# A long-convolution and MLP kernel: one filter block transformed by halves, two sums moved to accumulating DMAs, and a new instruction order

## The chip, the cores and the metric

The kernel runs on one core of one Trainium2 chip. The metric is the device time of one execution in microseconds. The kernel before took 238.65 us (median of three runs, 238.65 to 238.9).

A core has TensorE (PE; its weight loads are listed apart as PEld), VectorE (DVE), ScalarE (ACT), GpSimd (POOL) and SyncE (SP). They run side by side and wait for each other through semaphores. Plain DMAs are issued by SP here, and DMAs that add to what lies at the destination (accumulating DMAs) by POOL.

## The reference

The input is a sequence of 2048 tokens with 512 features, in bf16. Four layers follow each other, each added to its input: convolution, MLP, and the same two again with the same weights.

```python
def _A_ref(q, k, v, shift_k, ssm_k, ssm_D):
    ...
    for t in range(ks):                                    # ks = 4
        k_shift = k_shift + k_pad[:, t:t + S, :] * shift_k[:, ks - 1 - t][None, None, :]
    kv = k_shift * v
    ...                                                    # rfft over 2 S of kv and of ssm_k
    y_f = kv_f * kf_f[None, :, :, :]
    y = ...                                                # irfft, the first S tokens
    y = y + kv * ssm_D[None, None, :]
    return q * y

def _B_ref(x, w1, b1, w2, b2):
    y = _layernorm(x, axis=-1)
    h = _gelu(jnp.einsum("bsd,df->bsf", y, w1) + b1)       # 512 -> 1376
    return jnp.einsum("bsf,fd->bsd", h, w2) + b2

x = A_q
x = x + _A_ref(_layernorm(x, axis=-1), A_k, A_v, A_shift_k, A_ssm_k, A_ssm_D)
x = x + _B_ref(_layernorm(x, axis=-1), B_w1, B_b1, B_w2, B_b2)
x = x + _A_ref(_layernorm(x, axis=-1), A_k, A_v, A_shift_k, A_ssm_k, A_ssm_D)
x = x + _B_ref(_layernorm(x, axis=-1), B_w1, B_b1, B_w2, B_b2)
```

The convolution's result y depends on k, v and the filter only, not on x. So it is computed once and used in both layers.

## The kernel before

**Blocks.** The 2048 tokens are cut into four blocks of 512. Token t of a block lies on partition t // 4 in slot t % 4. The convolution is done block by block in the frequency domain: `spectrum_h(m)` makes the spectrum of filter block m (H0 to H3), `shift(b)` the short convolution of k and its product with v (S0 to S3), `forward` or `forward4` the spectrum of that (K0 to K3), `products(b)` the sum over j of X[j] times H[b-j] (P0 to P3), and `inverse(b)` the way back (Y0 to Y3). Each transform is a set of matmuls with a table of cosines and sines. Then `mlp(b, L)` follows for block b in layer L (called M00, M10, M01 and so on, block first): in its part a the normalisation, the gate with y and a second normalisation, in its part b the two matmuls with the gelu between.

**A transform in two ways.** `direct` makes each of four output tiles of 1024 columns from eight matmuls (four token slots, real and imaginary part, 512 columns each), and ScalarE's copy of a tile (`copy`, line 575) is the result. `forward` makes the even and the odd slots apart, with four matmuls a tile, and the results are the sum and the difference of two tiles: two more VectorE operations of 2048 elements when called with `whole`. Filter blocks 1 and 2 use `direct`, blocks 0 and 3 `forward`. The odd slots with the sign turned come from a copy of half the table that is negated once at the start (`negate`, line 636).

**Products.** A complex product is made of two multiplications on VectorE, one for the real and one for the imaginary part, each of 2048 elements (L569, the helper `tt`). The first term is written into the accumulator and each later term into one of three slots, from which an accumulating DMA of 512 KB (helper `accumulate`, L676) adds it. After the last term VectorE subtracts or adds the two halves of each sum and forms what the inverse transform reads.

`keep()` copies H1's spectrum (L730), then `wrap(m)` adds the block before to each filter spectrum: the real part on VectorE, the imaginary part by an accumulating DMA of 256 KB.

**The order.** The program lists some thousand operations with what they read and write. The tracker works in cells of four elements, and two operations that touch one cell of which one writes are put in order. An operation may have two possible engines: SIDE lists those that take their second choice. For copies of transposed tiles, the negation and the norms (`norm`, L860 on ScalarE, L861 on VectorE) the first choice is ScalarE and the second VectorE; for the small operations on statistics (`small`) it is VectorE and POOL. BANKS gives each PSUM tile its bank, and ORDER the order of all operations, from which each engine's own order follows. SIDE, BANKS and ORDER are the result of a search outside of the program with the durations written beside each operation; the chip takes from them only the order and the engines. `keep_busy` puts matmuls without a purpose (L1027) where that estimate has TensorE idle.

**Lines to follow.** L915: first matmul of an MLP, L920 its gelu, L949 (and L939) the second, L954 and L957 the residual sum, L829 and L831 statistics, L898 transposes ahead of an MLP, L591 all transforms, L714 the short convolution, L563 the transposition of short rows into columns, such as the bias b1. The row b1 is loaded to the start of `R_HT[0]`.

Of the kernel before, what the change touches and what calls it, by code (L numbers as in the profile page):

```python
# [366 lines left out]
def _tables():  # L367
# [8 lines left out]
SIDE = [27, 30, 36, 53, 118, 121, 129, 151, 220, 293, 300, 306, 364, 386, 496, 499, 517, 537, 581, 595, 730, 731, 741, 742, 752, 764, 827, 830, 844, 845, 848, 862, 866, 914, 915, 926, 929, 935, 936, 946, 947]  # L376
BANKS = "36424405320422044444020004461636165302046622145035042530020422242022432360231256613054243602540142362450404020024152406632314524121231045060153260200404000612503263500643350243511320451623164065313412554620212124626031532560"
ORDER = [
# [48 lines left out]
def bass_interleave_layers__ssm_conv_h3__mixer_channel_mlp__prompt_kernel(  # L427
        nc, A_q, A_k, A_v, A_shift_k, A_ssm_k, A_ssm_D, B_x, B_w1, B_b1, B_w2, B_b2, out):
    P = Prog(nc)
# [222 lines left out]
    def spectrum_h(m):  # L652
        o = R_BT + 4 * U * (m % 2)
        tl = Tile(P, 2)
        ins = [(i, c, A(0, 128, R_H[m] + c * U + i, [4, 128])) for i in range(4) for c in range(4)]

        def f(e, ins=ins, tl=tl):
            for i, c, src in ins:
                r = e.transpose(QB(tl, 0, 128, i * U + c * 128, [1, 128]), src, IDN)  # L659
            return r  # L660
        P.op(PE, f, 16 * 60.0, reads=[x[2] for x in ins] + [IDN], tile=tl)
        copy(A(0, 128, o, [1, 4 * U]), tl, lambda tl=tl: QB(tl, 0, 128, 0, [1, 4 * U]), 2048, (ACT, DVE), True)
        if m == 0:
            tt(A(0, 1, o, [1, U]), A(0, 1, o, [1, U]), A(0, 1, R_D, [1, U]), ALU.add, 512)
        if m in (1, 2):
            return direct(o, R_H[m])
        forward(o, R_H[m], (R_TMP, R_HT[0], R_EO[0], R_EO[0])[m], m > 0)
# [10 lines left out]
    def shift(b):  # L678
        kt = R_KT[b % 2]
        for z in range(2) if b == 0 else ():  # L680
# [8 lines left out]
            copy(A(0, 128, kt + 2 * 129 * z + 1, [4 * 129, 4], [129, 2], [1, 128]), tl, lambda tl=tl: QB(tl, 0, 128, 0, [256, 4], [128, 2], [1, 128]), 1024, (ACT, DVE), True)  # L689
        if b:  # L690
# [8 lines left out]
            copy(A(0, 128, kt + 1, [129, 16], [1, 128]), tl, lambda tl=tl: QB(tl, 0, 128, 0, [128, 16], [1, 128]), 2048, (ACT, DVE), True)  # L699
# [3 lines left out]
        for h in range(2):  # L703
            tl = Tile(P, 2)
            ins = []
            for z in range(2):
                c = 2 * h + z
                for m in (0, 1, 2, 3, -1, -2, -3):
                    ins.append((z * 512 + max(m, 0) * 128, A(0, 128, kt + (c * 4 + m % 4) * 129 + (m >= 0), [1, 128]),
# [31 lines left out]
    def products(b):  # L741

        for c in range(2):
# [15 lines left out]
            if b in ():  # L759
# [3 lines left out]
        for cs in ((0, 1),) if b else ((0,), (1,)):  # L763
            acc, n = R_ACC + cs[0] * 4096, len(cs)
            d = [[4096, 2]] if n == 2 else []
            for ri in range(1 if b in () else 2):
# [88 lines left out]
    def norm(b, i, mr, o):  # L855
# [6 lines left out]
        P.op((ACT, DVE), f, {ACT: 705.0, DVE: 330.0}, reads=[x, m, r], writes=[o])  # L862
# [195 lines left out]
```

## Time and profile before

| what | value |
|---|---|
| median of three runs | 238.65 us |
| the profiled execution | 238.38 us |
| its span, first to last instruction | 236.6 us |
| granted TensorE clock | 1.00 |
| VectorE 128x2048 bf16 sum or product (L569) | 1212 ns |
| ScalarE 128x1024 copy out of PSUM (L575) | 1030 ns |
| accumulating DMA, 512 KB and 256 KB, issue to landing | 5.4 and 4.3 us |

The profile is of one execution. A row of the chain of waits has a start, a length, and the engine and line that ran then. A row of the timeline has start and length of a run of like instructions, then engine, line, operation, output and input, count, and in brackets the idle time before it with what ended that. A row of the groups has the count, the busy time, the mean of one in ns, and the idle time before. The table by stage has the busy time and the number of instructions of PE, PEld, DVE, ACT and POOL, the granted clock, the busy share of DMA and its GB/s.

### The profile page before, as it was taken

To read this page: it belongs to the slowest core of one execution; us is meant where nothing else is said; L and a number is where in the kernel's file an instruction comes from. 1 tells how busy PE (TensorE), PEld (TensorE's weight loads), DVE (VectorE), ACT (ScalarE), POOL (GpSimd) and SP (SyncE) were. 2 spreads that over 40 slices of the span, in tenths; PEclk is the share of its full clock that TensorE was granted. 3 is DMA by queue.
4 is the path that set the end of the run, shared out by engine and by line. 5 is a ranking of instruction groups with operands and counts; after the bars stand their busy time and mean duration, and the time that the engine had idled before them with its cause. 6 is when DMAs were issued, how large, how long until landed. Compare 5 with 4: busy or idle time off the path is not lost.

```text
span 236.6 us, 3707 instructions
## 1 busy us (share of the span) xinstructions
PE 229.3 (97%) x1418; PEld 126.7 (54%) x1418; DVE 187.7 (79%) x366; ACT 168.0 (71%) x260; POOL 74.5 (31%) x93
## 2 busy tenths in 40 slices
PE   8999999999999999899999999899999999999995
PEld 4646645547746754345444544444457654447864
DVE  1669999999999999999999999789897414933022
ACT  2168779999999599989987965558938446815810
POOL 1000034257963454580367523334302101310000
PEclk9999999999999999999999999999999999999999
DMA  6999904989975987840299999940022220022016
GB/s 185 395 378 344 392 30 179 184 249 189 157 114 93 172 155 136 155 90 0 42 191 192 188 202 231 197 94 3 1 44 44 47 44 0 3 44 44 0 37 232
DMA packets 19865, 32.42 MB, mean 137 GB/s; under 512 B 7588, under 2 KB 13318, under 8 KB 19720
## 3 DMA queue, kind: packets, MB, share of 16 engines
q0 software_dynamic: 5808, 16.26, 36.4%
q1 hardware_dynamic: 14038, 15.93, 20.7%
q8 instruction: 11, 0.18, 0.3%
q14 instruction: 6, 0.05, 0.1%
q10 hardware_dynamic: 2, 0.00, 0.0%
HBM read 12.26 MB, written 2.10 MB: 61 GB/s over the span
## 4 chain that ended last, share of the span: by engine, by line
PE 55%; DVE 31%; DMA 6%; ACT 5%; issue 2%; DVEq 0%
DVE ar L569 22%; PE ps L949 21%; PE ps L915 18%; PE ps L591 7%; DMA ar<-ar 6%; DVE sm L829 5%; ACT ar L575 3%; PE ps L714 3%; PE ps L939 2%; PE ps L1027 2%; PE ps L659 1%; DVE ar L726 1%; ACT ar L920 1%; DVE ar L954 1%; DVE ar L957 1%
## 5 line engine op out<-in xcount | busy, mean ns | idle before, releaser
L569 DVE TENSOR_TENSOR ar<-ar 128x2048 bf16<-128x2048 bf16 (+2 forms) x129 | 115.4, 926 | 4.1 <-ACT ar L575 2.3
L915 PE MATMUL ps<-ar 128*128 128x256 bf16 (+3 forms) x484 | 80.1, 321 | 1.1 <-ACT ar L920 0.7
L920 ACT ACTIVATE ar<-ps,sm 128x256 bf16<-128x256 f32 (+3 forms) x121 | 61.4, 572 | 26.7 <-PE ps L915 26.4
L575 ACT ACTIVATE ar<-ps 128x1024 bf16<-128x1024 f32 (+2 forms) x61 | 63.7, 1098 | 17.9 <-PE ps L591 11.4
L949 PE MATMUL ps<-ar 128*128 128x512 bf16 (+1 forms) x330 | 75.7, 379 | 0.0
L915 PEld LDWEIGHTS ps<-ar 128*128 128x128 bf16 (+1 forms) x484 | 47.8, 100 | 32.5 <-ACT ar L920 1.4
L949 PEld LDWEIGHTS ps<-ar 128*128 128x128 bf16 (+1 forms) x330 | 31.9, 98 | 35.3 <-ACT ar L920 0.5
L676 POOL DMA_DIRECT2D ar<-ar x34 | 32.3, 1002 | 53.9 <-DVE ar L569 18.4
L591 PE MATMUL ps<-ar 128*128 128x512 bf16 x200 | 47.1, 379 | 1.0 <-DVE ar L726 0.5
L860 ACT ACTIVATE ar<-ar,sm 128x512 bf16<-128x512 bf16 x45 | 34.4, 808 | 7.5 <-DVE sm L818 7.4
L817 POOL TENSOR_TENSOR sm<-sm 128x2 f32<-128x2 f32 x32 | 29.1, 908 | 29.0 <-DVE sm L834 16.2
L829 DVE BATCH_NORM_STATS2 sm<-ar 128x6 f32<-128x512 bf16 x48 | 32.5, 685 | 1.7 <-DMA ar<-in_A_q_dram 1.5
L591 PEld LDWEIGHTS ps<-ar 128*128 128x128 bf16 x200 | 18.5, 98 | 24.0 <-ACT ar L575 2.3
L957 DVE TENSOR_TENSOR ar<-ps,ar 128x512 bf16<-128x512 f32 x14 | 9.6, 685 | 16.7 <-PE ps L949 16.6
L954 DVE SCALAR_TENSOR_TENSOR ar<-ps,ar 128x512 bf16<-128x512 f32 x16 | 10.9, 683 | 7.9 <-PE ps L949 7.8
L714 PE MATMUL ps<-ar 128*128 128x256 bf16 (+3 forms) x112 | 15.1, 288 | 0.3 <-DVE ar L576 0.3
L850 ACT ACTIVATE ar<-ar,sm 128x512 bf16<-128x512 bf16 x16 | 11.5, 722 | 4.3 <-DVE sm L846 4.1
L836 POOL TENSOR_SCALAR sm<-sm 128x2 f32<-128x2 f32 x4 | 3.7, 914 | 30.2 <-DVE sm L831 30.0
L714 PEld LDWEIGHTS ps<-ar 128*128 128x128 bf16 x112 | 9.6, 98 | 5.1 <-DVE ar L576 0.8
L846 POOL TENSOR_SCALAR sm<-sm 128x2 f32<-128x2 f32 x6 | 4.8, 792 | 12.2 <-DVE ar L954 11.9
L831 DVE BATCH_NORM_AGGREGATE sm<-sm 128x2 f32<-128x6 f32 x48 | 7.7, 172 | 0.2
L861 DVE TENSOR_SCALAR ar<-ar,sm 128x512 bf16<-128x512 bf16 x19 | 7.5, 408 | 0.2
(43 smaller groups left out, 78.2 us busy)
## 6 DMA issues: line engine op xcount, KB each, us to landing
ar<-ar POOLq DMA_DIRECT2D x24, 512.0 KB, 5.4
ar<-ar POOLq DMA_DIRECT2D x10, 256.0 KB, 4.3
ar<-in_A_ssm_k_dram SPq DMA_DIRECT2D x4, 512.0 KB, 10.3
ar<-in_A_v_dram SPq DMA_DIRECT2D x4, 512.0 KB, 5.7
ar<-in_A_q_dram SPq DMA_DIRECT2D x4, 512.0 KB, 10.1
ar<-in_A_k_dram SPq DMA_DIRECT2D x3, 512.0 KB, 7.4
out_dram<-ar SPq DMA_DIRECT2D x3, 512.0 KB, 3.7
ar<-in_B_w_dram SPq DMA_DIRECT2D x1, 1376.0 KB, 11.2
```

Of the source, the lines that this page charges most:

```text
L569: return P.op(DVE, lambda e: e.tensor_tensor(o, a, b, op), 66.0 + 0.52 * n, reads=[a, b], writes=[o])
L575: return e.activation(dst, src(), AF.Copy)
L591: r = e.matmul(Q(tl, 0, 128, ri * 512, [1, 512]), w, m, start=a, stop=z)
L676: P.op(POOL, lambda e: e.dma_start(dst, src, accum_op=ALU.add), 880.0, reads=[src, dst], writes=[dst], dma=True, nbytes=nb)
L714: r = e.matmul(Q(tl, 0, 128, q, [1, n]), w, d, start=a, stop=o)
L817: P.op(POOL, lambda e: e.tensor_tensor(r, v, hf, ALU.pow), 690.0, reads=[v, hf], writes=[r])
L829: P.op(DVE, lambda e, st=st, x=x: e.bn_stats(st, x), 600.0, reads=[x], writes=[st])
L860: return e.activation(o, x, AF.Identity, bias=m, scale=r)
L915: r = e.matmul(Q(tl, 0, rows, 0, [1, n]), w, m, start=dk == 0, stop=dk == 3)
L920: P.op(ACT, lambda e, dst=dst, tl=tl, rows=rows, bias=bias, n=n: e.activation(dst, Q(tl, 0, rows, 0, [1, n]), AF.Gelu_apprx_tanh, bias=bia ...
L949: r = e.matmul(Q(tl, 0, 128, 0, [1, 512]), ins[fc][0], ins[fc][1], start=fc == 0, stop=fc == 10)
L954: P.op(DVE, lambda e, x=x, tl=tl, mr=mr: e.scalar_tensor_tensor(x, Q(tl, 0, 128, 0, [1, 512]), 1.0, x, ALU.mult, ALU.add, accum_out=mr), 7 ...
```

## The change

Filter block 1 goes through `forward` instead of `direct`, with `R_HT[0]` as the place of the even and odd parts. For block 2 the sum of the two halves of the imaginary products is made by one accumulating DMA of 256 KB for each half of the frequencies, right behind that half's last product, in place of one VectorE addition of 2048 elements. The transposed k is laid by token slot first and column group second, where it was the other way round; the copies into it and the matmuls out of it follow. The duration of a norm on VectorE, as the search uses it, goes from 330 to 385 ns. SIDE, BANKS and ORDER are new; the numbers of the operations move with the added and removed ones.

```diff
-SIDE = [27, 30, 36, 53, 118, 121, 129, 151, 220, 293, 300, 306, 364, 386, 496, 499, 517, 537, 581, 595, 730, 731, 741, 742, 752, 764, 827, 830, 844, 845, 848, 862, 866, 914, 915, 926, 929, 935, 936, 946, 947]
+SIDE = [27, 51, 120, 131, 142, 153, 288, 305, 366, 388, 499, 517, 520, 584, 595, 606, 620, 733, 734, 745, 752, 755, 763, 766, 767, 833, 836, 854, 857, 858, 865, 868, 869, 917, 918, 932, 938, 939, 949, 950]
...
-        if m in (1, 2):
+        if m in (2,):
             return direct(o, R_H[m])
         forward(o, R_H[m], (R_TMP, R_HT[0], R_EO[0], R_EO[0])[m], m > 0)
...
-            copy(A(0, 128, kt + 2 * 129 * z + 1, [4 * 129, 4], [129, 2], [1, 128]), tl, lambda tl=tl: QB(tl, 0, 128, 0, [256, 4], [128, 2], [1, 128]), 1024, (ACT, DVE), True)
+            copy(A(0, 128, kt + 8 * 129 * z + 1, [129, 4], [4 * 129, 2], [1, 128]), tl, lambda tl=tl: QB(tl, 0, 128, 0, [256, 4], [128, 2], [1, 128]), 1024, (ACT, DVE), True)
...
-            copy(A(0, 128, kt + 1, [129, 16], [1, 128]), tl, lambda tl=tl: QB(tl, 0, 128, 0, [128, 16], [1, 128]), 2048, (ACT, DVE), True)
+            copy(A(0, 128, kt + 1, [129, 4], [4 * 129, 4], [1, 128]), tl, lambda tl=tl: QB(tl, 0, 128, 0, [512, 4], [128, 4], [1, 128]), 2048, (ACT, DVE), True)
...
-                    ins.append((z * 512 + max(m, 0) * 128, A(0, 128, kt + (c * 4 + m % 4) * 129 + (m >= 0), [1, 128]),
+                    ins.append((z * 512 + max(m, 0) * 128, A(0, 128, kt + (m % 4 * 4 + c) * 129 + (m >= 0), [1, 128]),
...
-            if b in ():
+            if b in (2,):
                 p, q = (A(0, 128, acc + 2048 + 512 * z, [1024, 2], [1, 512]) for z in range(2))
                 accumulate(p, q, 410000)
...
-            for ri in range(1 if b in () else 2):
+            for ri in range(1 if b in (2,) else 2):
                 p, q = (A(0, 128, acc + 2048 * ri + 512 * z, *d, [1024, 2], [1, 512]) for z in range(2))
...
-        P.op((ACT, DVE), f, {ACT: 705.0, DVE: 330.0}, reads=[x, m, r], writes=[o])
+        P.op((ACT, DVE), f, {ACT: 705.0, DVE: 385.0}, reads=[x, m, r], writes=[o])
```

More of the change, by code (lines that the diff above doesn't have):

```diff
@@ L373, in _tables @@
     return F.transpose(1, 0, 2, 3, 4).reshape(128, 2048), F.transpose(4, 2, 3, 0, 1).reshape(128, 2048) / 512
-SIDE = [27, 30, 36, 53, 118, 121, 129, 151, 220, 293, 300, 306, 364, 386, 496, 499, 517, 537, 581, 595, 730, 731, 741, 742, 752, 764, 827, 830, 844, 845, 848, 862, 866, 914, 915, 926, 929, 935, 936, 946, 947]
-BANKS = "36424405320422044444020004461636165302046622145035042530020422242022432360231256613054243602540142362450404020024152406632314524121231045060153260200404000612503263500643350243511320451623164065313412554620212124626031532560"
+SIDE = [27, 51, 120, 131, 142, 153, 288, 305, 366, 388, 499, 517, 520, 584, 595, 606, 620, 733, 734, 745, 752, 755, 763, 766, 767, 833, 836, 854, 857, 858, 865, 868, 869, 917, 918, 932, 938, 939, 949, 950]
+BANKS = "26424403120422040440042024260056342416310350522105601620040244242020261106404513132153164155521036001450404424024025555402536621364526035610402321444242200520245052163032651656442501653354104262100301532201443655366605256310"
 ORDER = [
[42 rows of a table removed]
[42 rows of a table added]
 ]
```

84 rows, old and new, of the table ORDER are left out of this document.

## The prediction

> **What bounds the kernel now.** I read the page first, then the chain of waits, then the table by stage, then who TensorE waits for, then the timeline at the joints.
>
> ```profile
> span 236.6 us, 3707 instructions
> ...
> PE 229.3 (97%) x1418; PEld 126.7 (54%) x1418; DVE 187.7 (79%) x366; ACT 168.0 (71%) x260; POOL 74.5 (31%) x93
> ```
>
> The chain that ended last goes: TensorE mixed with others to 33 us, VectorE to 91, TensorE to 131, VectorE and an accumulating DMA to 163, TensorE to the end. Two of its pieces:
>
> ```profile
> 147.72 7.50 DMA ar<-ar
> ...
> 195.75 9.50 PE ps L915 x44
> ```
>
> The last row gives the price of a matmul: 9.50 us / 44 = 0.216 us for 512 columns, with nothing between. Now the stages (first column: stretch, then its length, then busy time by engine):
>
> ```profile
> 33.00:98.00 65.00, 63.89 (x429) 36.55 (x426) 64.07 (x116) 59.90 (x85) 34.70 (x37) 1.00 0.77 157
> 98.00:132.00 34.00, 33.74 (x174) 15.87 (x175) 33.76 (x65) 29.34 (x46) 17.91 (x23) 1.00 0.58 109
> 132.00:164.00 32.00, 30.64 (x159) 14.30 (x158) 29.24 (x55) 20.89 (x33) 11.84 (x14) 1.00 0.77 159
> 164.00:234.00 70.00, 69.94 (x433) 42.35 (x431) 36.63 (x98) 39.31 (x82) 7.92 (x12) 1.00 0.17 43
> ```
>
> From 33 to 132 us TensorE and VectorE are both full; after 164 TensorE alone is, 69.94 of 70 us. So the time is TensorE's list of work plus the little it stands still. Two limits work at once: TensorE's total, and the joints where a convolution's products on VectorE (inverse transforms Y1, Y2, Y3) must be ready when TensorE's list comes to them. At each joint VectorE has just finished:
>
> ```profile
> 65.63 5.20 DVE L569 TENSOR_TENSOR ar<-ar 128x2048 bf16<-128x2048 bf16 x5
> ...
> 68.03 1.89 PE L591 MATMUL ps<-ar 128*128 128x512 bf16 x8
> ...
> 107.62 7.76 DVE L569 TENSOR_TENSOR ar<-ar 128x2048 bf16<-128x2048 bf16 x9
> ...
> 112.07 2.13 PE L591 MATMUL ps<-ar 128*128 128x512 bf16 x8
> ...
> 157.89 5.54 DVE L569 TENSOR_TENSOR ar<-ar 128x2048 bf16<-128x2048 bf16 x6
> ...
> 163.49 1.04 PE L591 MATMUL ps<-ar 128*128 128x512 bf16 x4
> ```
>
> Y1 starts at 68.03, right after the first two of the row from 65.63, block 1's last sums (2 x 1.2 us, to 67.95); Y2 at 112.07, inside the row from 107.62 (its first six instructions are block 2's sums); Y3 at 163.49, after the row that ends at 163.43.
>
> **The change part by part.** (a) *Filter block 1 by halves.* Four tiles of eight matmuls become four of four: 16 x 0.216 = 3.46 us less for TensorE, in the stretch of 25 to 33 us:
>
> ```profile
> 27.92 8.80 PE L591 MATMUL ps<-ar 128*128 128x512 bf16 x40
> ...
> 31.57 1.02 ACT L575 ACTIVATE ar<-ps 128x1024 bf16<-128x1024 f32 x1 [0.64 <-PE ps L591]
> ```
>
> ScalarE's copy of such a tile is 1.02 us and TensorE's eight matmuls 1.73 us, so ScalarE waited 0.64 us there; with 0.87 us a tile it no longer does. VectorE gains a sum and a difference of 2048 elements, two at 1.21 us (first row below): +2.42 us. The copy of the spectrum (keep) and block 1's wrap now wait for these two:
>
> ```profile
> L569 DVE TENSOR_TENSOR ar<-ar 128x2048 bf16<-128x2048 bf16 x60 | 71.5, 1212 | 1.9 <-DMA ar<-ar 1.3 <-ACT ar L575 0.5
> ...
> 34.64 0.76 POOL L730 DMA_DIRECT2D ar<-ar  x1 [1.52 <-ACT ar L575]
> ...
> 38.02 4.10 DVE L569 TENSOR_TENSOR ar<-ar 128x2048 bf16<-128x2048 bf16 x4 [0.47 <-ACT ar L575]
> ...
> 40.49 1.26 POOL L676 DMA_DIRECT2D ar<-ar  x1 [3.13 <-DMA ar<-ar]
> ...
> 48.02 1.21 DVE L569 TENSOR_TENSOR ar<-ar 128x2048 bf16<-128x2048 bf16 x1
> ```
>
> Keep issues at 34.64 now. In VectorE's new order the two sums stand just ahead of the K1 sums that begin at 38.02, so by estimate they end near 37 and keep issues 2.4 us later. The wrap follows keep by 40.49 - 34.64 = 5.85 us and its transfer of 256 KB takes 4.3 (a row under b): 37 + 5.85 + 4.3 = 47.2 us. Its first reader, block 1's product with this filter, begins at 48.02 and moves two places back. So it costs nothing, with 0.8 us of cover; from below it can't gain, and without the cover it is at most 2.4 - 0.8 = 1.6 us at Y1. The second wrap moves behind two small POOL operations of M00, and its reader stands eight VectorE operations after the first's: nothing.
>
> The intermediate lies where the row b1 is loaded, so two of the four tiles wait for b1's transposition, which the order moves ahead of them.
>
> ```profile
> 14.82 0.59 SPq L495 DMA_DIRECT2D ar<-in_B_b_dram  x2
> ...
> ar<-in_B_w_dram SPq DMA_DIRECT2D x1, 96.0 KB, 14.4
> ```
>
> b1 is issued by 15.4 us, right behind the 96 KB of W2 that took 14.4 us because of the 1280 KB ahead of them; the tiles come after 25 us. If b1 were as slow, 29.8 us, ScalarE would copy the other two tiles and H2's first: 0 to 1 us, I take 0.
>
> (b) *Block 2's imaginary sums.* One VectorE operation of 2048 elements goes, -1.21 us; two accumulating DMAs of 256 KB come.
>
> ```profile
> ar<-ar POOLq DMA_DIRECT2D x24, 512.0 KB, 5.4
> ar<-ar POOLq DMA_DIRECT2D x10, 256.0 KB, 4.3
> ...
> L676 POOL DMA_DIRECT2D ar<-ar x34: 853/902/1727, 40.5 to 153.0; - x34
> ...
> 95.62 0.87 POOL L676 DMA_DIRECT2D ar<-ar  x1 [2.07 <-DVE sm L852]
> ...
> 100.42 0.94 POOL L676 DMA_DIRECT2D ar<-ar  x1 [1.61 <-DMA ar<-ar]
> ...
> 106.37 1.22 DVE L569 TENSOR_TENSOR ar<-ar 128x2048 bf16<-128x2048 bf16 x1
> ```
>
> They are issued between the accumulates at 95.62 and 100.42, and ahead of the latter on POOL. Each waits for an accumulate that is issued before the one at 95.62, whose landing releases 100.42 anyway. The issues take 2 x 0.90 = 1.8 us, of which the 1.61 us idle there hides most. Queued behind are a small POOL operation of M20 and the accumulate of 100.42, and for it waits the real sum at 106.37, hence Y2. That accumulate lands near 100.42 + 5.4 = 105.8 us, 0.6 before VectorE came to it. What two transfers of 256 KB add to the flight of their neighbours no row shows: from 0 (they fit between; no less, as they add work) to their own 4.3 us; I take 1 us, near the low end, since the stage rows show DMA busy 0.77 and 0.58 of the time on both sides of 98 us.
>
> [...]
>
> (c) *Transposed k by token slot.* The same copies with other strides. The strided bf16 copy and the plain one cost the same (1018 against 1030 ns below), so nothing. It separates the two halves of block 0's k, which the tracker's cells of four elements joined; VectorE's 0.4 us wait for ScalarE's half (the 1024 copies' row) goes, in the start where TensorE has fillers to run.
>
> ```profile
> L575 ACT ACTIVATE ar<-ps 128x1024 bf16<-128x1024 f32 x46 | 45.6, 1030 | 13.0 <-PE ps L591 11.4 <-PE ps L714 1.4
> ...
> L575 ACT ACTIVATE ar<-ps 128x1024 bf16<-128x1024 bf16 x10 | 10.0, 1018 | 4.9 <-PE ps L686 3.4 <-PE ps L898 1.4
> ...
> L575 ACT ACTIVATE ar<-ps 128x2048 bf16<-128x2048 bf16 x5 | 9.4, 1883 | 0.0
> ...
> L576 DVE COPY ar<-ps 128x2048 bf16<-128x2048 bf16 x2 | 2.4, 1224 | 1.8 <-PE ps L659 1.8
> ...
> L576 DVE COPY ar<-ps 128x1024 bf16<-128x1024 bf16 x2 | 1.4, 688 | 0.4 <-ACT ar L575 0.4
> ...
> L636 DVE TENSOR_SCALAR ar<-ar 128x1024 bf16<-128x1024 bf16 x1 | 0.4, 416 | 0.0
> ...
> 13.29 1.02 ACT L575 ACTIVATE ar<-ps 128x1024 bf16<-128x1024 f32 x1 [6.23 <-PE ps L591]
> ...
> ACT ar L575 <- PE ps L591: 10.3, 9, 6.2
> ```
>
> (d) *The list of second choices (SIDE).* I matched old and new operation numbers (98 to 472 move up by two, 473 to 483 by three or four, later ones by three). Two copies of 2048, one copy of 1024 and the negation leave VectorE for ScalarE: VectorE -2 x 1.22 - 0.69 - 0.42 = -3.55 us, ScalarE about 2 x 1.88 + 2 x 1.02 = +5.8 us. Norms trade places one for one but for one, which ScalarE loses (0.8 us). VectorE in sum: 2.42 - 1.21 - 3.55 = -2.3 us, nearly all before Y3. ScalarE's gain is covered: one long copy and the negation fall in its 6.23 us wait before 13.29, the rest in the other 4.1 us that it waited for L591 up to 75 us. Without that cover it would be 2 us at Y1.
>
> (e) *The order.* On SP load_k of block 3 moves one place up, the transposing pairs swap, and the stores of blocks 1 and 2 go ahead of the last ones; the last store still follows the last sum, so nothing there. On TensorE Y2's halves now have one M01 tile (0.87 us) between them. Y3 stands behind nine M11 tiles as before.
>
> **The sum.** TensorE's 3.46 us can't all arrive, since the joints hold it. At Y2, VectorE has about 1.7 us less work ahead, but the accumulate landing near 105.8 allows 0.6 us, plus what its own chain gains (0 to 1.7, I take 1) less the 1 us of (b): 0.6. With the M01 tile that TensorE has done meanwhile, 1.5 us. After Y2 TensorE stood 32.0 - 30.64 = 1.4 us before 164, partly for M11's norm behind this row:
>
> ```profile
> 150.27 1.29 DVE L829 BATCH_NORM_STATS2 sm<-ar 128x6 f32<-128x512 bf16 x2 [1.51 <-DMA ar<-in_A_q_dram]
> ...
> 153.22 0.62 PE L898 MATMUL ps<-ar 128*128 128x128 bf16 x8 [0.96 <-ACT ar L860]
> ```
>
> The store and then load of that q start after a residual sum that moves two places up, and M11's norm now uses both engines; half of the 1.4 returns, 0.7. Sum 1.5 + 0.7 = 2.2 us; after Y3 the full stretch of 70 us is the same work. The profiled run took 238.38 us (span 236.6, 1.8 around it), 0.3 under the median of 238.65. Span 234.4, run 236.2, against the median 236.4 us.
>
> **Rivals.**
> 1. *TensorE's whole saving arrives.* 3.46 us, plus 0.5 of the 1.4: 238.65 - 4.0 = 234.7. For it: TensorE is full in every stage and VectorE is relieved too. Against: the three joints above.
> 2. *Nothing arrives; VectorE's joints set all.* Y3 comes when it came, as the accumulates chain (7.50 us for one at 147.72) is not shortened: gain 0 to 0.8, 238.2. [...]
> 3. *Slower.* The two new accumulates, ahead of the accumulate of 100.42 on POOL, delay it by d, and Y2 with it; TensorE has little else listed before Y2 and stands. The forecast has d = 1 and its chain 1 us earlier by VectorE's relief, so the gain is 3.2 - d: it decides from d = 3.2 us. At the dear end nothing of the issue is hidden and the flight is added whole, d = 1.8 + 4.3 = 6.1 us: 241.5. Halfway between, d = 4.65: 238.65 + 1.45 = 240.1. Against: POOL's idle 1.61 us hides most of the issue, and DMA has room.
>
> **How the numbers follow.** Forecast (235.4 to 237.6) 0.45; rival 1 0.20; rival 2 0.15; rival 3 0.20. A change under 0.2%, 0.48 us, can't be told from none. Rival 2 gives 0.05 to faster and 0.10 to same: faster 0.70, same 0.10, slower 0.20. The range 234.2 to 240.2 leaves out the far ends of rivals 1 and 3, under 0.2.
>
> **What would show it.** Right: sixteen fewer L591 matmuls, VectorE about 185.4 us busy, ScalarE near 173, Y2 0 to 1.5 us earlier than 112.07, Y3 about 2 earlier than 163.49, TensorE full after it. Wrong: TensorE waiting over 2 us at Y1 or Y2 for VectorE or a DMA (rivals 2, 3), VectorE waiting for an accumulate near 105 us, or new holes after Y3.

## The result and the profile after

The changed kernel takes 241.8 us (median of five, 241.41 to 242.48) where the kernel before takes 238.65 (238.4 to 238.9): a ratio of 1.0136, 95% interval 1.0118 to 1.0154. That is 3.2 us slower. The forecast was 236.4 us and the range ended at 240.2, so both were wrong. The profiled execution took 241.8 us, its span is 240.1, 3.5 us more than before.

From the page of the changed kernel: busy times, the transforms (L591; the row of the kernel before stands last), and the 256 KB accumulating DMAs.

```profile
PE 228.8 (95%) x1402; PEld 125.0 (52%) x1402; DVE 185.8 (77%) x362; ACT 172.5 (72%) x263; POOL 81.0 (34%) x97
...
L591 PE MATMUL ps<-ar 128*128 128x512 bf16 x184 | 43.7, 380 | 3.2 <-ACT ar L575 2.3
...
ar<-ar POOLq DMA_DIRECT2D x12, 256.0 KB, 4.7
...
L591 PE MATMUL ps<-ar 128*128 128x512 bf16 x200 | 47.1, 379 | 1.0 <-DVE ar L726 0.5
```

The work changed as the prediction had it: VectorE 185.8 us (185.4 forecast), ScalarE 172.5 (173), TensorE 1402 matmuls for 1418. The busy time of the transforms fell by 3.4 us, as forecast. TensorE's busy time in sum fell by 0.5 us only, since that of the MLP's second matmuls (L949) went from 75.7 to 78.1 us, 1.2 us of it in eight that ran while the clock was low (3.11 us from 77.60; eight in new_wraps, at a clock of 1.00, took 1.89). What made the kernel slower is the time in which TensorE stood. The table by stage shows where, first before and then after (columns as in the prediction's table):

```profile
17.00:40.00 23.00, 23.00 (x161) 12.58 (x159) 22.39 (x40) 19.48 (x20) 3.66 (x5) 1.00 0.72 254
40.00:81.00 41.00, 40.50 (x290) 24.87 (x288) 41.00 (x64) 38.14 (x52) 22.91 (x22) 1.00 0.82 160
98.00:164.00 66.00, 64.37 (x331) 30.16 (x332) 63.00 (x119) 50.23 (x78) 29.75 (x36) 1.00 0.67 133
```

```profile
17.00:40.00 23.00, 21.33 (x151) 10.94 (x150) 22.80 (x38) 21.90 (x22) 4.99 (x6) 1.00 0.60 211
40.00:81.00 41.00, 35.78 (x228) 19.50 (x226) 35.90 (x57) 34.21 (x43) 23.50 (x21) 0.96 0.76 159
76.00:80.00 4.00, 3.23 (x14) 1.75 (x15) 3.84 (x6) 3.78 (x6) 2.38 (x3) 0.58 0.30 52
98.00:164.00 66.00, 66.00 (x341) 31.32 (x340) 64.00 (x127) 53.09 (x84) 33.32 (x38) 1.00 0.78 152
```

TensorE stands 1.7 us in 17 to 40 us (before: nothing) and 5.2 in 40 to 81 (before 0.5), and from 76 to 80 us its clock is at 0.58. From 98 us on it is full, where it stood 1.6 us before. So in this run the joints that the prediction watched, Y2 and Y3, cost nothing, and all of the loss is made before 81 us. A full stretch behind a late one does not show that the joints were mended: in the repaired kernel fix (below), which comes there earlier, TensorE stands again, 1.61 us at 157.38. VectorE lost as much there: 35.90 of 41 us busy, where it was full before.

The chain of waits of the changed kernel (start, length, what) names the place:

```profile
36.92 4.88 DMA ar<-ar
...
42.11 8.82 DMA ar<-ar
...
50.95 2.36 DVE ar L569 x2
...
62.83 4.72 POOL sm L836
...
67.62 1.68 POOL sm L817
...
76.77 1.04 PE ps L898 x8
```

Keep (36.92) and W1's first accumulate (42.11) are on it, and then two tiny POOL operations on statistics, one of them 4.72 us long for 128x2 values. The timelines of POOL and VectorE in that stretch:

```profile
60.69 2.05 POOL L676 DMA_DIRECT2D ar<-ar  x2 [2.03 <-DVE ar L569]
62.83 4.71 POOL L836 TENSOR_SCALAR sm<-sm 128x2 f32<-128x2 f32 x1
67.62 1.68 POOL L817 TENSOR_TENSOR sm<-sm 128x2 f32<-128x2 f32 x1
69.26 3.73 POOL L676 DMA_DIRECT2D ar<-ar  x3
73.07 0.19 POOL L834 TENSOR_SCALAR sm<-sm 128x2 f32<-128x2 f32 x1
73.34 0.72 POOL L817 TENSOR_TENSOR sm<-sm 128x2 f32<-128x2 f32 x1
```

```profile
62.78 4.68 DVE L569 TENSOR_TENSOR ar<-ar 128x1024 bf16<-128x1024 bf16 x5
67.38 0.17 DVE L831 BATCH_NORM_AGGREGATE sm<-sm 128x2 f32<-128x6 f32 x1
...
74.09 0.16 DVE L818 SCALAR_TENSOR_TENSOR sm<-sm 128x2 f32<-128x2 f32 x1 [2.75 <-POOL sm L817]
```

POOL began its operations in this order: M10's small pair (62.83, 67.62), then three accumulates of W2 and W3 (69.26), then M00's pair (73.07, 73.34). VectorE stands 2.75 us for the last one, ScalarE's norm follows, and TensorE stands 2.45 us before the transposes of 76.77. In the kernel before, this pair of M10 runs earlier, at 54.89. Then come two of the accumulates, the pair of M10's second half, the other two accumulates, and M00's pair:

```profile
59.69 2.44 POOL L676 DMA_DIRECT2D ar<-ar  x2 [0.25 <-DVE ar L569]
61.17 1.35 POOL L836 TENSOR_SCALAR sm<-sm 128x2 f32<-128x2 f32 x1
...
64.30 2.49 POOL L676 DMA_DIRECT2D ar<-ar  x2
66.87 1.14 POOL L834 TENSOR_SCALAR sm<-sm 128x2 f32<-128x2 f32 x1
```

### The profile page after: what moved, and what is told of

It reads as the page before. It is cut to its first block, busy times and chain, and to the rows that moved or that the text cites. A ratio compares the mean times of both kernels' runs of the same rounds, so it can differ in the third digit from the quotient of the medians.

```text
span 240.1 us, 3676 instructions
## 1 busy us (share of the span) xinstructions
PE 228.8 (95%) x1402; PEld 125.0 (52%) x1402; DVE 185.8 (77%) x362; ACT 172.5 (72%) x263; POOL 81.0 (34%) x97
## 4 chain that ended last, share of the span: by engine, by line
PE 67%; DVE 15%; DMA 6%; POOL 5%; ACT 4%; issue 1%
PE ps L949 29%; PE ps L915 27%; DVE ar L569 12%; DMA ar<-ar 6%; ACT ar L575 3%; PE ps L591 3%; PE ps L714 2%; POOL ar L676 2%; PE ps L939 2%; POOL sm L836 2%; PE ps L898 2%; PE ps L1027 1%; POOL sm L817 1%; DVE sm L829 1%; ACT ar L860 1%
## 5 line engine op out<-in xcount | busy, mean ns | idle before, releaser
L569 DVE TENSOR_TENSOR ar<-ar 128x1024 bf16<-128x1024 bf16 (+2 forms) x130 | 116.0, 931 | 6.0 <-DMA ar<-ar 3.1
L949 PE MATMUL ps<-ar 128*128 128x512 bf16 (+1 forms) x330 | 78.1, 383 | 0.0
L575 ACT ACTIVATE ar<-ps 128x1024 bf16<-128x1024 f32 (+2 forms) x64 | 68.4, 1119 | 13.3 <-PE ps L686 3.7
L676 POOL DMA_DIRECT2D ar<-ar x36 | 35.3, 1054 | 48.3 <-DVE ar L569 31.7
L949 PEld LDWEIGHTS ps<-ar 128*128 128x128 bf16 (+1 forms) x330 | 32.2, 99 | 35.6 <-issue 1.6
L591 PE MATMUL ps<-ar 128*128 128x512 bf16 x184 | 43.7, 380 | 3.2 <-ACT ar L575 2.3
L817 POOL TENSOR_TENSOR sm<-sm 128x2 f32<-128x2 f32 x32 | 32.8, 1024 | 24.0 <-DVE sm L834 11.5
L591 PEld LDWEIGHTS ps<-ar 128*128 128x128 bf16 x184 | 16.6, 98 | 26.1 <-ACT ar L575 5.8
L836 POOL TENSOR_SCALAR sm<-sm 128x2 f32<-128x2 f32 x7 | 9.7, 1387 | 27.0 <-DVE sm L831 26.6
L714 PEld LDWEIGHTS ps<-ar 128*128 128x128 bf16 x112 | 9.6, 98 | 6.9 <-ACT ar L575 1.8
L818 DVE SCALAR_TENSOR_TENSOR sm<-sm 128x2 f32<-128x2 f32 x32 | 4.9, 152 | 6.5 <-POOL sm L817 6.5
L898 PE MATMUL ps<-ar 128*128 128x128 bf16 x80 | 6.4, 228 | 2.5 <-ACT ar L860 2.5
## 6 DMA issues: line engine op xcount, KB each, us to landing
ar<-in_B_w_dram SPq DMA_DIRECT2D x1, 1376.0 KB, 10.3
```

Of the source, the lines that this page charges most:

```text
L569: return P.op(DVE, lambda e: e.tensor_tensor(o, a, b, op), 66.0 + 0.52 * n, reads=[a, b], writes=[o])
L575: return e.activation(dst, src(), AF.Copy)
L591: r = e.matmul(Q(tl, 0, 128, ri * 512, [1, 512]), w, m, start=a, stop=z)
L676: P.op(POOL, lambda e: e.dma_start(dst, src, accum_op=ALU.add), 880.0, reads=[src, dst], writes=[dst], dma=True, nbytes=nb)
L714: r = e.matmul(Q(tl, 0, 128, q, [1, n]), w, d, start=a, stop=o)
L817: P.op(POOL, lambda e: e.tensor_tensor(r, v, hf, ALU.pow), 690.0, reads=[v, hf], writes=[r])
```

## The experiments

All kernels are timed beside the kernel before, whose medians there were 238.38 to 238.61 us. Those named new change only the order (or SIDE) of the changed kernel; those named old are the kernel before with parts of the change; those named fix are repaired. In all, no group of matmuls without a purpose is begun behind the first 16 places of TensorE's order, where both kernels have theirs.

| run | us | ratio to before, 95% interval |
|---|---|---|
| changed kernel | 241.8 | 1.0136, 1.0118 to 1.0154 |
| new_pool | 244.25 | 1.0246, 1.0205 to 1.0287 |
| new_both | 244.4 | 1.0265, 1.0222 to 1.0309 |
| new_port | 240.65 | 1.0101, 1.0057 to 1.0144 |
| new_wraps | 238.62 | 1.0014, 0.9990 to 1.0037 |
| new_load | 240.62 | 1.0095, 1.0067 to 1.0124 |
| new_side | 243.46 | 1.0212, 1.0179 to 1.0244 |
| old_a | 240.93 | 1.0094, 1.0059 to 1.0129 |
| old_a2 | 242.3 | 1.0164, 1.0133 to 1.0195 |
| old_b | 238.33 | 0.9999, 0.9979 to 1.0019 |
| old_side | 242.07 | 1.0135, 1.0105 to 1.0166 |
| old_all | 245.43 | 1.0271, 1.0236 to 1.0306 |
| fix | 237.68 | 0.9958, 0.9941 to 0.9975 |
| fix_norm | 238.12 | 0.9983, 0.9965 to 1.0002 |
| fix_direct | 240.41 | 1.0075, 1.0047 to 1.0104 |

In the diffs of orders, numbers are those of the new ORDER: 274 and 276 are W3's accumulates, 280 and 278 W2's, 366 and 367 M10's first small pair (L836, L817), 153 and 154 M00's second (L834, L817).

### POOL's order between 61 and 74 us

**new_pool.** POOL's part of ORDER:

```diff
-274, 366, 367, 280, 276, 278, 153, 154
+274, 366, 367, 153, 154, 280, 276, 278
```

> The changed kernel, but on POOL the two small operations of M00's second half (L836 and L817 at 73.07 and 73.34 us) go ahead of three of the four accumulates of the wraps W2 and W3 (issued from 69.26 to 72.99). Theory 1 (the loss is POOL's order: TensorE's 2.6 us at 76.77 stand behind these accumulates, and its low clock follows from the standstill): the wait before the transposes of 76.77 goes, granted clock near 1.00 in 76 to 80 us, time 2.5 to 4 us below the changed kernel, 237.8 to 239.3. Theory 2 (block 1 by halves makes keep and the wraps late, and everything behind them): the wait only moves to the next product that reads W2 or W3, time 241 to 242. Theory 3 (the two new accumulates of block 2): nothing here touches them, 241.4 to 242.

It became slower still. TensorE's transposes no longer wait (they run at 73.95), but the accumulates now come later, and VectorE stands for one of them:

```profile
76.64 1.29 DVE L569 TENSOR_TENSOR ar<-ar 128x1024 bf16<-128x1024 bf16 x2 [3.71 <-DMA ar<-ar]
```

So theory 1 in its narrow form falls: the statistics aren't alone in being late, everything in that queue is, and whatever stands last pays. Theory 2 named the place of the wait rightly, and not the time. A part of the time may be the clock's: it was at 0.986 in three of the four executions (0.993 in the changed kernel).

**new_both.** Also M10's pair ahead of an accumulate:

```diff
-25, 249, 251, 274, 366, 367, 280, 276, 278, 153, 154
+25, 366, 367, 249, 251, 274, 153, 154, 280, 276, 278
```

> As the run before, and M10's first small pair (L836 for 4.71 us from 62.83, L817 for 1.68) goes ahead of the accumulate issued at 57.82. Theory 1: the 4.71 us operation falls to 1 to 2 us, VectorE's 0.62 us wait at 69.34 and TensorE's 1.0 us before Y1 at 70.69 go too: 0.5 to 1.5 us below the run before, 236.5 to 238.5. Theory 2: no change against it.

The small operation still took 3.97 us (56.38 to 60.35), under another run of VectorE sums, and the product whose slot a delayed accumulate frees waited 2.52 us. Both theories missed. So POOL's order is not the whole cause of the 4.71 us, and what VectorE does at the time comes into question.

**new_port.** One VectorE statistics operation (152) moves up past four sums:

```diff
-451, 469, 253, 273, 252, 152
+451, 152, 469, 253, 273, 252
```

> The changed kernel, with one VectorE statistics operation of 0.17 us (M00's second half, at 67.38) moved five places up on VectorE, between the sums that begin at 62.78 and 63.37. Theory 1a (POOL's 4.71 us operation at 62.83 does not compute but waits until VectorE runs something else than a two-operand sum or product): it ends near 63.7, POOL's three accumulates and M00's statistics come 3 to 5 us earlier, TensorE's waits at 70.69 and 76.77 and VectorE's at 69.34 and 74.09 go, the clock stays at 1.00: 236.5 to 238.5. [...]

VectorE and POOL with this edit:

```profile
63.76 0.17 DVE L831 BATCH_NORM_AGGREGATE sm<-sm 128x2 f32<-128x6 f32 x1
63.85 5.32 DVE L569 TENSOR_TENSOR ar<-ar 128x2048 bf16<-128x2048 bf16 x5
```

```profile
63.21 0.71 POOL L836 TENSOR_SCALAR sm<-sm 128x2 f32<-128x2 f32 x1
64.00 4.50 POOL L817 TENSOR_TENSOR sm<-sm 128x2 f32<-128x2 f32 x1
68.46 3.73 POOL L676 DMA_DIRECT2D ar<-ar  x3
```

The operation that took 4.71 us ends at 63.92, when the moved one runs on VectorE. The next on POOL then meets the rest of the sums and takes 4.50 us, though L817 takes 0.72 when VectorE stands (73.34 above). So at this place the small POOL operation waits out VectorE's run of two-operand sums (it ran from 64.00 to 68.50 us, the sums from 63.85 to 69.17). The expected time was not reached, since the delay only passed to the next operation; the 0.8 us under the changed kernel lie within the two intervals. The wait is not as long everywhere: in the kernel before, L834 and L817 took 1.14 and 1.04 us (66.87 above, and 68.09) under the five sums that the prediction shows at 65.63. What decides whether one sum or most of a run is waited out, no run here shows.

**new_wraps.** On POOL all four accumulates come first and both pairs behind them. On VectorE the W3 sum (273) goes ahead of 469 and a small operation (368) behind 254; on ScalarE a K2 copy (462) goes ahead of M10's norms.

```diff
-274, 366, 367, 280, 276, 278, 153, 154
+274, 280, 276, 278, 366, 367, 153, 154
```

> The changed kernel, with POOL's order as the kernel before has it: all four accumulates of W2 and W3 first, then M10's small pair, then M00's; the W3 sum that the last of them needs goes one place ahead on VectorE, and M10's norm and its copy trade places so that nobody stands behind the pair. Theory 1b (the order of POOL's queue from 61 to 74 us is the loss): 236.5 to 238.5, no TensorE wait over 1.5 us after 57 us and clock 1.00. Theory 2 (lateness from keep and W1): 240.5 to 242.

Theory 1b holds: 1.0014 for 1.0136, so 1.22% or 2.9 us, in the expected direction and 0.1 us over the top of the expected band. It is the worth of all these moves together; those on VectorE and ScalarE were not tried apart from POOL's. POOL and TensorE:

```profile
60.74 5.78 POOL L676 DMA_DIRECT2D ar<-ar  x5 [2.02 <-DVE ar L569]
66.60 0.99 POOL L836 TENSOR_SCALAR sm<-sm 128x2 f32<-128x2 f32 x1
67.67 1.69 POOL L817 TENSOR_TENSOR sm<-sm 128x2 f32<-128x2 f32 x1
69.52 0.44 POOL L834 TENSOR_SCALAR sm<-sm 128x2 f32<-128x2 f32 x1 [0.16 <-POOL sm L817]
```

```profile
74.73 0.62 PE L898 MATMUL ps<-ar 128*128 128x128 bf16 x8 [1.14 <-ACT ar L860]
```

The last accumulate of the five is issued by 66.5 us instead of 73.0, M00's pair starts at 69.52 instead of 73.07, and TensorE stands 1.14 us, not 2.45, with its clock at 1.00 all through.

### The loads on top of W1's accumulate

**new_load.** SP's order; 445 is the load of block 2's q, which waits for nothing, 498 a load that waits until 41.10:

```diff
-498, 445, 260, 444
+445, 498, 260, 444
```

> The changed kernel, with one load of 512 KB (q of M10) put ahead of the load that waits until 41.10 us, so that three and not four loads fall on W1's first accumulate (8.82 us). Theory 2 (contention with the loads makes W1 late, and this the rest): the accumulate lands 1.2 us earlier or more, VectorE's 1.56 us wait at 50.95 shrinks as much, and the time falls by as much or more: 240 to 240.8. Theory 1 (POOL's order at 61 to 74): the wait there shrinks, but the one at 74 stays: 241 to 242.

1.0095 for 1.0136, 1.0 us. W1's first accumulate is issued at 42.26 and lands at 49.77, 7.5 us for 8.82, and VectorE's wait there falls from 1.56 to 0.12 us. TensorE's 2.45 us at the transposes stay. Theory 2 is right for this piece and theory 1 for the rest: two losses, one behind the other. SP's timeline of the changed kernel and of the kernel before shows the four and the three loads:

```profile
19.11 0.88 SPq L495 DMA_DIRECT2D ar<-in_A_q_dram  x1
41.10 0.33 SPq L495 DMA_DIRECT2D ar<-in_A_k_dram  x1
41.47 0.43 SPq L495 DMA_DIRECT2D ar<-in_A_q_dram  x1
41.95 0.91 SPq L495 DMA_DIRECT2D ar<-in_A_v_dram  x2
```

```profile
20.30 0.43 SPq L495 DMA_DIRECT2D ar<-in_A_q_dram  x1
44.19 0.33 SPq L495 DMA_DIRECT2D ar<-in_A_k_dram  x1
44.56 1.03 SPq L495 DMA_DIRECT2D ar<-in_A_v_dram  x2
```

Before, W1's first accumulate had landed at 44.34, as the loads began. Now keep is later, the loads earlier, and there is one more of them.

### ScalarE's added copies

**new_side** gives the copies and the negation back to VectorE in the changed kernel, **old_side** puts the new SIDE into the kernel before.

```diff
-SIDE = [27, 51, 120, ...]
+SIDE = [27, 30, 36, 51, 53, 120, ..., 222, ...]
```

> The changed kernel, with the three copies of transposed tiles and the negation back on VectorE (SIDE gains 30, 36, 53 and 222). Theory 4 (ScalarE has too much: TensorE's 2.9 us of waits from 17 to 40 us): these waits fall under 1 us, VectorE has 3.55 us more: 239.5 to 241. Theories 1 and 2: VectorE later by 1 to 3 us at Y1, 241.5 to 244.

> The kernel before, in its own order, with only the new second choices of engines. My prediction's step (d) (ScalarE's 5.8 us are covered, VectorE's 3.55 us are worth up to their size): 236.5 to 238.5. Theory 4 (ScalarE is full from 17 to 62 us and hands its lateness to TensorE): 239 to 241.

Both directions cost. new_side is 1.8 us over the changed kernel (1.0212 for 1.0136), in the band of theories 1 and 2. old_side is 3.2 us over the kernel before, 1 us above theory 4's band. It has four more matmuls without a purpose, 0.9 us, ahead of S0's third tile; that tile still waits 0.48 us for a copy behind them, so they don't set its start. In 17 to 40 us new_side's TensorE stands 1.9 us (busy 21.07 of 23), no less than the changed kernel's 1.7: it waits for VectorE there, 1.3 us in one piece. In old_side TensorE's waits are spread: in sum 1.5 us before transforms for ScalarE's copies, 1.4 for a norm on VectorE, 1.4 for gelus, and smaller ones. So theory 4 has the sign right in the old order, with the copies shown as a part of the loss only, and it fails in the new one. That each order is fitted to its own split would explain both runs; it was not tried.

### The parts alone, in the order of the kernel before

**old_a** and **old_a2**: only block 1 by halves; in old_a its sums stand ahead of block 0's last product sums, in old_a2 behind them.

```diff
-        if m in (1, 2):
+        if m in (2,):
```

> The kernel before, in its own order and second choices, with only block 1 by halves: its two new VectorE sums stand right ahead of keep, b1's transposition ahead of the second tile. Theory 1 (the work is less, the new order loses it): 235.5 to 238. Theory 2 (keep 2 to 3 us later, W1's first accumulate among the loads of 44 us, VectorE and then Y1 wait for it): 239.5 to 241.5, with a wait of over 1 us at block 1's first product with that filter.

> The kernel before with only block 1 by halves, as the run old_a, but the two VectorE sums stand behind all sums of block 0's product and keep behind M00's small operation, so that Y0 no longer waits for them. Theory 6 (from 33 to 98 us VectorE is full and passes the 2.42 us on): no TensorE wait over 2 us, yet 1 to 2.5 us above the kernel before, 239.5 to 241. Rival (old_a was slower only by the misplaced sums and the clock): 236 to 238.

Both are slower. old_a's time lies in theory 2's band, but not for its reason: VectorE does not wait at the product with W1's filter. TensorE stands before Y0 instead, and its clock drops (timeline, then a stretch by stage):

```profile
39.32 4.28 PE L591 MATMUL ps<-ar 128*128 128x512 bf16 x12 [2.23 <-DVE ar L569]
```

```profile
39.00:46.00 7.00, 6.68 (x35) 3.35 (x36) 6.94 (x13) 4.49 (x5) 3.31 (x3) 0.76 0.59 168
```

Its two executions whose clock stayed at 1.00 took 238.35 and 238.77 us, the eight others 239.73 to 241.81: in those two, without the drop of the clock, the halves in the old order give nothing and cost nothing. old_a2 has no TensorE wait over 2 us, and is slower by more than theory 6 expected. There keep comes at 38.93 us, and W1's first accumulate, issued 1.3 us later than in old_a (43.88 for 42.58), lands 4.6 us later (51.08 for 46.44), now among the loads; VectorE waits for it:

```profile
51.10 1.23 DVE L569 TENSOR_TENSOR ar<-ar 128x2048 bf16<-128x2048 bf16 x1 [1.84 <-DMA ar<-ar]
```

**old_b**: only block 2's imaginary sums by accumulating DMAs.

```diff
-            if b in ():
+            if b in (2,):
...
-            for ri in range(1 if b in () else 2):
+            for ri in range(1 if b in (2,) else 2):
```

> The kernel before, in its own order, with only block 2's imaginary sums by two accumulating DMAs, issued right ahead of the accumulate of 100.42 us. Theory 1 and my prediction: 238 to 239, Y2 within 1 us of 112.07. Theory 3 (their issue and flight delay the accumulate behind them and Y2): 240 to 241.5, Y2 2 us or more later and TensorE standing there.

Nothing, 0.9999. The three issues in a row and the real sum behind them:

```profile
98.78 3.43 POOL L676 DMA_DIRECT2D ar<-ar  x3
```

```profile
107.24 1.23 DVE L569 TENSOR_TENSOR ar<-ar 128x2048 bf16<-128x2048 bf16 x1 [0.78 <-DMA ar<-ar]
```

The sum waits 0.78 us and starts at 107.24 for 106.37. Theory 3 falls.

**old_all**: the whole new program and the new SIDE in the old order (12 instead of 13 matmuls without a purpose).

> The changed program (block 1 by halves, block 2's accumulates, the new layout of k) with the new second choices of engines, but in the order of the kernel before, with the new operations put in as in old_a2 and old_b. If the order alone is at fault and the program would have paid as predicted: 235.5 to 237.5. If the program needs an order of its own, since block 1's sums and the later keep hit joints that were set without them: 239 to 242, with waits of VectorE or TensorE for W1's accumulate between 45 and 60 us.

245.43 us: the program needs an order of its own. VectorE waits 2.04 us for W1's accumulate at 52.90, and TensorE stands in every stage. The new order loses 2.9 + 1.3 us, and it is still 3.2 us better (1.0136 for 1.0271) for this program than the old one with the new operations put in by hand.

### Repaired

**fix** is new_wraps and new_load together; **fix_norm** also moves both norms of M00's second half ahead of Y1's first copy; **fix_direct** is fix with filter block 1 directly again.

> The changed kernel with both repairs: POOL's order of the kernel before for W2, W3 and the two small pairs, and the load of 512 KB put ahead. Theory 5 (the two losses add: 3.2 us and 1.2 us of 241.8): 237.2 to 237.8, a little under the kernel before. Rival (they are one loss, seen twice): 238.4 to 239.

> As the run before, and on ScalarE both norms of M00's second half go ahead of Y1's first copy and M10's norms, the gate product of M10 one product later on VectorE: the transposes of M00a1 stop waiting (1.30 us at 74.73 in the repaired order). If TensorE's waits alone set the time: 0.8 to 1.3 us below the run before, 236 to 237. If VectorE's products set it from here to Y2: no change.

> As the run labelled fix, but filter block 1 directly again: 3.46 us more for TensorE, two VectorE sums (2.42 us) less, keep 2.4 us earlier. My prediction's step (a) (TensorE's 3.46 us are mostly worth having): 1 to 3 us above the run fix. Theory 6 (at 17 to 40 us ScalarE paces, so that TensorE waits there for as much as it saves, and VectorE has the sums on top): within 0.5 us of the run fix or below it.

fix is at 0.9958, 0.56% or 1.3 us below new_wraps: the two losses add, and this version is 0.9 us faster than the kernel before. fix_direct lies 1.17% or 2.8 us above fix, so in this order block 1 by halves is worth most of its 3.46 us, and theory 6 falls there. The order was made for the halves, though: in fix_direct VectorE stands 4.61 us at 39.48 for ScalarE's copies, and how much of the 2.8 us is that misfit is open. fix_norm is not faster than fix: the wait before the transposes (1.16 us in fix) is gone, but right behind it, at 75.66, TensorE stands 0.91 us for a copy of ScalarE. The wait was passed on, and the run doesn't show whether TensorE's waits there set the time. What still holds fix up shows in two places of its profile, which is of its slowest execution (238.32 us; the median is 237.68). Its chain of waits goes through ScalarE's copies, long after the last of the moved ones (before 22 us):

```profile
42.00 1.91 ACT ar L575
...
53.42 4.51 ACT ar L575 x4
```

and its VectorE waits for an accumulate of block 3's product, with TensorE standing 1.61 us soon after:

```profile
155.27 1.22 DVE L569 TENSOR_TENSOR ar<-ar 128x2048 bf16<-128x2048 bf16 x1 [2.20 <-DMA ar<-ar]
```

## Why the prediction was wrong

**The work (a, b, d): right.** VectorE's and ScalarE's totals came out within 0.5 us of the estimates. Step (a), TensorE's 3.46 us, holds: the transforms lost 3.4 us, and 2.8 us of time arrive in the repaired order, which was made for the halves. Step (b), d = 1 us, held too: 0.87 us at the real sum and nothing in the time; rival 3 named the right sign with the wrong mechanism. Step (c) was never run alone, and what it is worth is open.

**The wrap, "so it costs nothing, with 0.8 us of cover": wrong by its price.** Keep was issued at 36.92 as forecast (near 37), but the wrap was priced at the 4.3 us median of all 256 KB accumulates. Moved by 1.6 us it met four loads, which came 3.1 us earlier than before (41.10 for 44.19); it took 8.82 us and landed at 50.93, not 47.2. VectorE stood 1.56 us.

**Step (e), "nothing on SP": wrong, and the failed step.** I noted that a load of k moved one place up and took that for free. Passing it the other way, the load of q went from 20.30 to 41.47 us, behind a load that waits. With the wrap this is the 1.3 us between new_wraps and fix. Worse, no step walked POOL's queue from 61 to 74 us: step (a) named two small operations of M00 ahead of the second wrap, step (b) the issues near 100 us. There M10's pair stands ahead of three accumulates, right under a run of VectorE sums, and M00's pair behind them: 2.9 us, by new_wraps. Both are terms that the sum left out; together 4.2 of the 5.4 us between 236.4 and 241.8.

**Step (d), "ScalarE's gain is covered": wrong.** I set 5.8 us of copies against 6.23 + 4.1 us in which ScalarE waited. But that waiting shrank by more than the copies: from 10.3 us before to 1.1 in the changed kernel, since block 1's halves take some of it too (4.9 us are left in fix_direct, 2.4 in fix; all from 13 to 75 us). TensorE, which had hardly waited for a copy at its transforms, now does. A row of the waits has who waited for whom, the us in total, the times, and the longest; here the kernel before, the changed kernel and fix_direct:

```profile
PE ps L591 <- ACT ar L575: 0.3, 1, 0.3
...
PE ps L591 <- ACT ar L575: 2.3, 8, 0.4
...
PE ps L591 <- ACT ar L575: 2.0, 6, 0.4
```

Since 2.0 us stand in fix_direct too, the halves are not the main cause of these waits. How the rest, 237.68 in fix against 236.4, divides between these waits and the accumulate at 155 us was not tried.

**The stall after Y2, half of which was to return (0.7 us).** It is gone in the changed kernel, where 98 to 164 us is full and TensorE stands 1.6 us less, but there TensorE comes late to the stretch. In fix 1.61 us of standing is back at 157.38, so the 0.7 us is not shown as a gain. Y2 starts at 117.24 us and Y3 at 166.90, 5.2 and 3.4 us later than before, and the sign that the prediction gave for TensorE, a wait of over 2 us at Y1 or Y2, did not come: it waits 0.84 us at Y1 and not at Y2, and its wait of 2.45 us stands at M00's transposes, where the prediction did not look.

## What to carry to other kernels

A new order is not priced by counting work per engine: walk each engine's queue, in its order, past every moved operation, POOL's and SP's first, and ask for each what now stands in front of it and what that one waits for. A transfer that is moved is priced by what flies at its new time, not by the median of its kind. And a part of a change that is measured in the wrong order shows the order: block 1 by halves was worth 2.8 us in one and nothing or less in another.

## What the runs showed of the hardware

**POOL under VectorE's sums.** A POOL operation on 128x2 values took 0.19 us with VectorE idle (the row of 73.07), and another 4.71 us under five VectorE sums (62.83 in the changed kernel; 4.72 at the same place in new_pool). In new_port it ended after 0.71 us, while one VectorE operation of 0.17 us stood between the sums. Under five sums of the kernel before two such operations took 1.14 and 1.04 us, so it was not always that long.

**TensorE's clock.** After TensorE stood 2.23 us (old_a) and 2.45 us (changed kernel) the granted clock fell: it was 0.76 from 39 to 46 us in old_a and 0.50 from 77 to 80 us in the changed kernel, and there the eight transposes at 76.77 took 1.04 us, for 0.62 in new_wraps. In the profiled executions of new_port, where TensorE stood 2.03 us in sum from 72 to 82 us, and of new_side, where it stood 2.58 us in sum from 75 to 85, it stayed at 1.00. The stretch of new_side:

```profile
75.00:85.00 10.00, 7.42 (x57) 4.67 (x55) 8.94 (x12) 7.98 (x13) 6.21 (x8) 1.00 0.74 125
```

The price differs: 2.6 us in old_a (median 241.2 of the eight executions with a drop, 238.6 of the two without), 1.9 in new_port (242.41 in the one with a drop, median 240.55 of the three others), and in the changed kernel next to none, since its one execution at 1.00 took 241.55 us. So the clock is not the cause of the changed kernel's loss. What decides whether such a gap lowers the clock, no run here shows.
